# A recurrent-attention and expert kernel: the gate's count of every fourth chunk behind the block product instead of ahead of the scores

## Chip, cores, metric

One core of one Trainium2 chip. The metric is the device time of one execution in microseconds (us); lower is better. The inputs are fixed; the output is a float32 array of 3072 x 320.

## What is computed

Three stages follow one another. The first is a recurrence over 768 steps for 32 (batch, head) pairs with a 40 x 40 state; its output is 3072 tokens of 320 features. The second sends each token to the best of 8 experts (with a capacity), two matrix products per expert. The third is a dense layer pair with a squared ReLU. Cut to what matters:

```python
for t in range(S):                       # S = 768, state is B x H x 40 x 40
    y[:, :, t] = einsum('bhd,bhde->bhe', rt, state)
    Sa = einsum('bhde,bhe->bhd', state, at)
    state = state * wt[:, :, None, :] - einsum('bhd,bhe->bhde', Sa, bt) \
            + einsum('bhd,bhe->bhde', vt, kt)
...
expert_idx = argmax(x @ w_gate, axis=1)  # and gate_w, its softmax weight
# token i goes to place counts[e] of its expert e, in order of i
...
h = maximum(disp @ w1[e], 0); y = h @ w2[e]; out[i] = gate_w[i] * y[e, pos[i]]
...
h = maximum(x @ w_in, 0); return (h * h) @ w_out
```

## The kernel before, in words

The recurrence is done in 24 chunks of 32 steps (`Attention.run`). A chunk's coefficients form 32 x 32 triangular blocks, one for each of the 32 pairs, that have to be inverted. Their inverse is built by VectorE for four chunks at once, in pieces that are laid into the chunks between other work (`inv`, L265 and L269), and ends with a transpose into `TT` (L304). The index m = c % 4 tells a chunk's place in such a group; in the fourth chunk (m = 3) the inverse is ready and the next group's first block is taken from it.

All engines issue in the order in which the program is written (a manual schedule). `chunk(c)` (L585) is the body for chunks 1 to 19. The names that matter here, in the order of one chunk:

- `u(c)`: 32 small products into `pu` (L399), four copies to `vu` by ScalarE (L404).
- `y(c - 1)`: the last chunk's output into the PSUM tile `py` (L489).
- `nat_k(c + 1)` (L341, `pk`) and `gram(c + 7)`: the Gram products `G` (L192) of a chunk seven ahead, which VectorE masks into `GM` and `N` (L205, L206).
- `state(c)` (L418, `ps`) and `vu_t(c)`: transposes `pv` (L455) and two copies to `vut` by ScalarE (L458).
- `block_T(c + 1)`: four copies `TB` from `TT` by ScalarE (L313). In the fourth chunk they stand behind `vu_t`, since `TT` is made only then.
- `gate.count` of a batch of chunks: an exponential (L895), four matmuls into the PSUM tile `pc` (L899; the profile shows eight pieces), a copy to `pr` (L901).
- `scan` and `scale` (coefficients of chunk c + 8: two scans on VectorE, three products on POOL, L178), `state_decay(c)` (L429), `gate_in(c - 1)`: VectorE reads `py` and writes the token rows `xt` (L498).
- `scores(c)`: 16 matmuls into `pq` (L467; 32 pieces), masked by VectorE (`scores_mask`, L475).
- `solve(c + 1)`: the block product `px` of `TB` and `X` (L385), and two copies to `lu` by ScalarE (L388), which the next chunk's `u` needs.
- `gate.xT(c - 1)`: transposes `gpt` of `xt` (L845) and copies `gxT` (L847); `nat_a` (`pa`, L341), `state_t` (`pn`, L441), `gate.logits` (`pl`, L861).
- on VectorE at the end: pieces of the inverse (m below 3), or the rank of a batch of tokens (L908 to L938), which needs `pr`.

Batches for the gate are chunks 0-1, 2-5, 6-9, 10-13, 14-16 and later ones; a batch's count comes two chunks behind its last chunk, so for the first four it is in chunks 3, 7, 11 and 15, all with m = 3. In those it is called ahead of the scan (`early`); the later ones stand behind `gate.xT` already.

PSUM tiles come from two pools. Large ones (`pu`, `pk`, `G`, `ps`, `pv`, `px`, `pa`, `pn`) take three buffers in turn. Small ones (`py`, `pc`, `pq`, `gpt`, `pl`) take two buffers in turn, in the order in which they are asked for:

```python
def small(self, nm):
    self.ns += 1
    return self.ps1.tile([128, 512], F32, tag=f"s{self.ns % 2}", name=nm)
```

A tile can be written only when the last reader of the tile before it in that buffer has ended. The functions that the change touches, and what calls them:

Of the kernel before, what the change touches and what calls it, by code (L numbers as in the profile page):

```python
# [35 lines left out]
class Attention:  # L36
# [476 lines left out]
    def run(self, extra, weights):  # L513
# [3 lines left out]
        gate = self.gate  # L517

        def fill(c, i):
            if 1 <= c <= 2:  # L520
                extra(5 * c + i, 5 * c + i + 1)
            elif 5 <= c < 14 and i == 2:
                extra(10 + c, 11 + c if c < 13 else None)

        def wload(i):
            r = (self.L, self.Tt)[i % 2].rearrange("p a b -> p (a b)")
            weights.load(i, r[:, 0:704], 1)
# [57 lines left out]
        def chunk(c):  # L585

            m, bt = c % 4, gate.batch(c)
            plan = FIRST if c < 4 else PLAN
            early, nxt = bt if c < 17 else None, gate.batch(c + 1) if c < 16 else None
            self.u(c)  # L590
            if bt and 17 <= c:
                gate.choose(*bt)
            self.y(c - 1)
            self.nat_k(c + 1)
            if m != 3:
                self.block_T(c + 1)
            self.load_r(c + 1)
            self.load(c + LA + 2, 0)
            fill(c, 0)
            self.gram(c + LA)  # L600
            self.gram_mask(c + LA)
            self.state(c)
            self.vu_t(c)
            if m == 3:
                self.block_T(c + 1)
            self.load(c + LA + 2, 1)
            fill(c, 1)
            if early:
                gate.count(*early)
            self.scan(c + LA + 1)  # L610
            self.scale(c + LA + 1)
            self.state_decay(c)
            self.gate_in(c - 1)
            self.scores(c)
            self.scores_mask(c)
            if m == 0:
                self.inv_start(c // 4 + 1, lambda k, h: G)
            self.solve(c + 1)
            self.load_v(c + 2)
            self.store_x(c - 1)  # L620
            self.load_w(c + LA + 4)
            self.load(c + LA + 2, 2)
            fill(c, 2)
            gate.xT(c - 1)
            if bt and 17 <= c:
                gate.count(*bt)
            self.nat_n(c + 2)
            self.nat_a(c + 2)
            self.nat_pc(c + 2)
            self.state_t(c + 1)  # L630
            self.load(c + LA + 2, 3)
            fill(c, 3)
            gate.logits(c - 1)
            if m != 3:
                self.inv("v" * plan[m])
            if nxt:
                gate.choose(*nxt)
            if m == 2:
                self.inv("v" * plan[3])
            if bt:  # L640
                gate.rank(*bt)
                gate.rank_batch(*bt)
            fill(c, 4)
            gate.scatter(1)
            if c == 19:
                wload(0)
                wload(1)
# [5 lines left out]
        for c in range(NC - 1):  # L653
            if 1 <= c < SHIFT:
                chunk(c)
                continue
# [1014 lines left out]
```

## Time and profile before

| | |
|---|---|
| median of 3 runs | 1120.45 us (1119.92 to 1125.08) |
| the profiled execution | 1126.1 us, its span 1124.2 us |
| instructions in it | 30643 |
| mean granted TensorE clock | 0.904 of full speed |
| busy share: PE, DVE, ACT, POOL | 83%, 69%, 50%, 24% |
| chain that ended last: PE, DVE, DMA, issue, ACT | 54%, 18%, 6%, 6%, 5% |

PE is TensorE's matmul stream, DVE VectorE, ACT ScalarE. Busy shares are means over all of it. The chain follows the end back through what released each step; "issue" is time in which the engine waited for nothing that the profile shows. A row of the timeline gives the start and length in us, the engine, the line and what it writes and reads; several equal instructions in a row are merged (x32), and the bracket tells how long the engine was idle before and what released it. A wait for several things is put down to the one that came last by the profile, which can be the wrong one.

### The profile page before, as it was taken

How to read it: one execution, taken by the hardware profiler on the slowest of the kernel's cores; microseconds unless marked ns; L12 is line 12 of the kernel's file. 1: busy time of each engine (PE TensorE's matmuls, PEld its weight loads, DVE VectorE, ACT ScalarE, POOL GpSimd, SP SyncE). 2: the span in 40 equal slices, each digit the busy share in tenths (PEclk: the TensorE clock that was granted, in tenths of full speed). 3: DMA queues.
4: the chain of work that ended last, by engine and by line, in shares of the span. 5: the costliest groups of instructions: out<-in, count | busy, mean ns of one | idle time of the engine just before them, and what ended most of it. 6: DMA issues, size and time to landing. Idle time of an engine off the chain costs nothing.

```text
span 1124.2 us, 30643 instructions
## 1 busy us (share of the span) xinstructions
PE 934.6 (83%) x12526; PEld 842.7 (75%) x12526; DVE 774.2 (69%) x1611; ACT 560.4 (50%) x1286; POOL 273.8 (24%) x320
## 2 busy tenths in 40 slices
PE   5247677778666788889889999799999999999995
PEld 3237566667665677768879999798899999999895
DVE  7999979889798795465887888876644344444432
ACT  7135464555463767634545566546634343434432
POOL 5422131222313101013554555423401010000000
PEclk6578888797797988899989999999999999999998
DMA  7736544444442223236765666534100001000000
GB/s 184 194 97 184 172 125 124 124 140 149 115 149 84 87 61 104 79 93 181 222 209 187 208 212 216 178 98 143 50 24 24 24 12 37 1 24 2 19 5 27
DMA packets 80647, 122.71 MB, mean 109 GB/s; under 512 B 9679, under 2 KB 57409, under 8 KB 79561
## 3 DMA queue, kind: packets, MB, share of 16 engines
q1 hardware_dynamic: 71173, 100.09, 30.2%
q10 hardware_dynamic: 7020, 12.78, 3.8%
q0 software_dynamic: 2304, 7.78, 2.2%
q8 instruction: 101, 1.65, 0.6%
q14 instruction: 49, 0.40, 0.1%
HBM read 91.36 MB, written 29.35 MB: 107 GB/s over the span
## 4 chain that ended last, share of the span: by engine, by line
PE 54%; DVE 18%; DMA 6%; issue 6%; ACT 5%; POOL 1%; SPq 1%; ACTq 0%; DVEq 0%; POOLq 0%
PE phg L1334 15%; PE phe L1334 5%; PE pog L1359 5%; PE pog L1360 5%; PE pog L1358 5%; DVE pr L265 4%; PE px L385 3%; DMA xs<-zs_s 2%; PE pq L467 2%; PE poe L1360 2%; PE poe L1358 2%; PE poe L1359 2%; DVE Tt L269 1%; DVE ru L429 1%; DVE Xm L269 1%
## 5 line engine op out<-in xcount | busy, mean ns | idle before, releaser
L1344 DVE SCALAR_TENSOR_TENSOR sqg<-phg,rg 128x512 f32<-128x512 f32 x96 | 66.2, 690 | 119.0 <-ACT rg L1343 119.0
L1343 ACT ACTIVATE rg<-phg 128x512 f32<-128x512 f32 x96 | 57.2, 596 | 110.5 <-PE phg L1334 110.3
L1346 DVE TENSOR_TENSOR hlg<-sqg,hhg 128x512 fp32r<-128x512 f32 x96 | 66.5, 693 | 65.9 <-ACT hhg L1345 63.2
L1345 ACT CAST hhg<-sqg 128x512 fp32r<-128x512 f32 x96 | 59.6, 621 | 78.5 <-DVE sqg L1344 78.5
L1334 PE MATMUL phg<-xhg,e 128*128 128x512 f32 x264 | 93.1, 393 | 0.0
L385 PE MATMUL px<-TB,X 128*104 128x128 f32 x384 | 67.2, 347 | 26.2 <-ACT TB L313 25.0
L388 ACT COPY lu<-px 104x512 f32<-104x512 f32 x48 | 25.7, 588 | 120.5 <-PE px L385 120.5
L385 PEld LDWEIGHTS px<-TB,X 128*104 128x104 f32 x384 | 61.7, 230 | 28.8 <-ACT TB L313 25.4
L467 PE MATMUL pq<-rq,vut 128*64 128x64 f32 x768 | 42.1, 264 | 49.0 <-issue 31.7
L178 POOL TENSOR_TENSOR e<-e 104x512 f32<-104x512 f32 x21 | 27.9, 1331 | 207.4 <-DVE e L163 90.2
L467 PEld LDWEIGHTS pq<-rq,vut 128*64 128x64 f32 x768 | 35.7, 173 | 55.0 <-issue 32.2
L1359 PE MATMUL pog<-e,hhg 128*128 128x320 f32 x240 | 74.1, 309 | 0.0
L1360 PE MATMUL pog<-e,hlg 128*128 128x320 f32 x240 | 74.1, 309 | 0.0
L1358 PE MATMUL pog<-e,hhg 128*128 128x320 f32 x240 | 73.9, 308 | 0.0
L192 PE MATMUL G<-e 64*32 64x64 f32 (+1 forms) x1536 | 27.6, 254 | 49.3 <-issue 29.2
L192 PEld LDWEIGHTS G<-e 64*32 64x32 f32 (+1 forms) x1536 | 20.1, 120 | 59.3 <-issue 33.6
L1152 POOL TENSOR_TENSOR e<-rw,e 128x256 fp32r<-128x256 f32 x51 | 43.0, 846 | 72.3 <-ACT e L1151 71.5
L1334 PE MATMUL phe<-xhe,e 128*128 128x480 f32 (+4 forms) x176 | 59.3, 378 | 0.0
L178 POOL TENSOR_TENSOR e<-e,wB 104x512 f32<-104x512 f32 x42 | 53.4, 1287 | 24.3 <-DVE wB L157 17.1
L1334 PEld LDWEIGHTS phg<-xhg,e 128*128 128x128 f32 x264 | 49.5, 188 | 8.8
L313 ACT COPY TB<-TT 32x256 f32<-32x256 f32 x94 | 37.8, 402 | 35.6 <-DVE TT L304 34.3
L1338 ACT ACTIVATE hhe<-phe 128x480 fp32r<-128x480 f32 (+4 forms) x64 | 33.9, 529 | 38.7 <-PE phe L1334 38.2
(315 smaller groups left out, 2919.5 us busy)
## 6 DMA issues: line engine op xcount, KB each, us to landing
e<-in_E_dram ACTq DMA_DIRECT2D x60, 208.0 KB
rw<-in_w_dram SPq DMA_DIRECT2D x30, 320.0 KB
zs_s<-zt SPq DMA_DIRECT2D x24, 320.0 KB
rw<-in_w_dram SPq DMA_DIRECT2D x30, 256.0 KB
e<-in_E_dram SPq DMA_DIRECT2D x9, 832.0 KB
ru<-in_VR_dram SPq DMA_DIRECT2D x48, 128.0 KB
cr<-in_wi_dram SPq DMA_DIRECT2D x20, 256.0 KB
cr<-in_wo_dram SPq DMA_DIRECT2D x20, 256.0 KB
```

Source lines behind the costliest of these rows:

```text
L178: eng.tensor_tensor(z, z, f, ALU.mult)
L192: T.matmul(gps[32 * g : 32 * g + 32, par, 64 * o : 64 * o + 64], e[r, 32 * i : 32 * i + 32], e[r, 512 + 64 * i : 576 + 64 * i], start=True ...
L385: self.nc.tensor.matmul(px[0:104, par, 128 * o : 128 * o + 128], X[:, par, o, :], TB[:, 4 * par + o, :], start=True, stop=True)
L467: T.matmul(pq[s, 64 * q : 64 * q + 64], vut[:, q, s], rt[:, :, q, pp], start=True, stop=True)
L1334: T.matmul(o, lt, rt, start=(i == 0), stop=(i == len(seq) - 1))
L1343: A.activation(r[:, :n], o, AF.Relu)
L1344: V.scalar_tensor_tensor(sq[:, :n], o, 0.0, r[:, :n], ALU.max, ALU.mult)
L1345: A.copy(hh[:, :n], sq[:, :n])
L1346: V.tensor_tensor(hl[:, :n], sq[:, :n], b32(hh)[:, :n], ALU.subtract)
L1358: T.matmul(o, hh[:, t], W["h2"], start=(f == 0), stop=False)
L1359: T.matmul(o, hh[:, t], W["l2"], start=False, stop=False)
L1360: T.matmul(o, hl[:, t], W["h2"], start=False, stop=(f == NF - 1))
```

## The change

The call of `gate.count` for the batches of chunks 3, 7, 11 and 15 moves from ahead of `scan` to behind `solve`. Nothing else is edited.

```diff
--- before.py
+++ after.py
@@ -605,8 +605,6 @@
                 self.block_T(c + 1)
             self.load(c + LA + 2, 1)
             fill(c, 1)
-            if early:
-                gate.count(*early)
             self.scan(c + LA + 1)
             self.scale(c + LA + 1)
             self.state_decay(c)
@@ -616,6 +614,8 @@
             if m == 0:
                 self.inv_start(c // 4 + 1, lambda k, h: G)
             self.solve(c + 1)
+            if early:
+                gate.count(*early)
             self.load_v(c + 2)
             self.store_x(c - 1)
             self.load_w(c + LA + 4)
```

TensorE in chunk 11, from the end of `vu_t` to the transposes of the gate. `pc6` is the count, `pq11` the scores, `px12` the block product, `gpt10` the transposes; the brackets name what an instruction waits for. Before:

```order
L455 MATMUL pv11_4353<-ident0_59,vu1_115 80x64 [waits PE_49,Activation_49]
L455 MATMUL pv11_4353<-ident0_59,vu1_115 80x64 x15
L899 MATMUL pc6_4378<-oh_412,mats_384 128x32 [waits DVE_49]
L899 MATMUL pc6_4378<-oh_412,mats_384 128x32 x3
L467 MATMUL pq11_4397<-rq1_119,vut_117 64x64 [waits DMAHW0_49,DMAHW6_49,DVE_49,Activation_49]
L467 MATMUL pq11_4397<-rq1_119,vut_117 64x64 [waits Activation_49]
L467 MATMUL pq11_4397<-rq1_119,vut_117 64x64 x14
L385 MATMUL px12_4416<-TB0_110,X0_106 104x128 [waits PE_49,Activation_49]
L385 MATMUL px12_4416<-TB0_110,X0_106 104x128 x7
L845 MATMUL gpt10_4436<-ident0_59,xt10_4395 128x128 [waits Activation_49]
```

Now:

```order
L455 MATMUL pv11_4353<-ident0_59,vu1_115 80x64 [waits PE_49,Activation_49]
L455 MATMUL pv11_4353<-ident0_59,vu1_115 80x64 x15
L467 MATMUL pq11_4389<-rq1_119,vut_117 64x64 [waits DMAHW6_49,DMAHW0_49,Activation_49]
L467 MATMUL pq11_4389<-rq1_119,vut_117 64x64 [waits Activation_49]
L467 MATMUL pq11_4389<-rq1_119,vut_117 64x64 x14
L385 MATMUL px12_4408<-TB0_110,X0_106 104x128 [waits DVE_49,PE_49,Activation_49]
L385 MATMUL px12_4408<-TB0_110,X0_106 104x128 x7
L899 MATMUL pc6_4420<-oh_412,mats_384 128x32 [waits DVE_49]
L899 MATMUL pc6_4420<-oh_412,mats_384 128x32 x3
L845 MATMUL gpt10_4436<-ident0_59,xt10_4387 128x128 [waits DVE_49,PE_49]
```

The count's four matmuls stand behind the block product. The first scores matmul no longer waits for VectorE (`DVE`); the block product, the count and the first transpose of the gate do, each for a buffer or an operand.

ScalarE in the same chunk, from the last copies of `TB` on. Before:

```order
L313 COPY TB0_110<-TT_109 32x8x32 [waits DVE_49]
L313 COPY TB0_110<-TT_109 32x8x32 x3
L138 DMA e4_4282<-in_E_dram 104x512 [waits DMAHW2_49]
L895 ACTIVATE ex_6_4177<-d_6_4176 128x32
L901 COPY pr_6_4383<-pc6_4378 128x128 [waits PE_49]
L388 COPY lu_116<-px12_4416 104x512 [waits PE_49,Activation_49]
L388 COPY lu_116<-px12_4416 104x512 [waits Activation_49]
L138 DMA e4_4282<-in_E_dram 104x512 [waits DMAHW0_49]
L847 COPY gxT10_4440<-gpt10_4436 128x256 [waits PE_49]
```

Now:

```order
L313 COPY TB0_110<-TT_109 32x8x32 [waits DVE_49]
L313 COPY TB0_110<-TT_109 32x8x32 x3
L138 DMA e4_4282<-in_E_dram 104x512 [waits DMAHW2_49]
L388 COPY lu_116<-px12_4408 104x512 [waits PE_49,Activation_49]
L388 COPY lu_116<-px12_4408 104x512 [waits Activation_49]
L895 ACTIVATE ex_6_4177<-d_6_4176 128x32
L901 COPY pr_6_4425<-pc6_4420 128x128 [waits PE_49]
L138 DMA e4_4282<-in_E_dram 104x512 [waits DMAHW6_49]
L847 COPY gxT10_4440<-gpt10_4436 128x256 [waits PE_49]
```

The exponential (`ex`) and the counts' copy (`pr`) stand behind the two copies of the block product (`lu`), and ahead of a load's issue (L138) and of the copies of the gate's transposes (`gxT`). The orders of VectorE, POOL and SP have the same rows as before, in the same places.

## Rows read from the trace of the kernel before

**Rows 1.** One line of the kernel, L901 (the copy of the counts): who waited for it.

```profile
  PE pq L467: 28.7, 4
```

**Rows 2.** Timeline, chunk 11: start us, us, engine, line, operation, xcount [idle before <-releaser].

```profile
280.17 1.07 ACT L458 COPY vut<-pv 80x512 f32<-80x512 f32 x2 [2.01 <-PE pv L455]
...
282.95 1.23 ACT L313 COPY TB<-TT 32x256 f32<-32x256 f32 x3
...
287.77 0.49 DVE L498 TENSOR_TENSOR xt<-py,Pn 128x320 f32<-128x320 f32 x1
...
288.36 1.97 PE L467 MATMUL pq<-rq,vut 128*64 128x64 f32 x32 [6.81 <-issue]
...
290.26 3.63 PE L385 MATMUL px<-TB,X 128*104 128x128 f32 x16
...
290.37 1.39 DVE L475 TENSOR_TENSOR rq<-pq,mQ 64x512 f32<-64x512 f32 x2 [2.11 <-PE pq L467]
...
293.73 0.49 PE L845 MATMUL gpt<-ident,xt 128*128 128x128 f32 x3
...
295.90 0.80 PE L399 MATMUL pu<-ru,lu 128*32 128x40 f32 x64
```

**Rows 3.** Timeline, chunk 12, which has no count: scores and gate_in.

```profile
305.48 1.15 PE L467 MATMUL pq<-rq,vut 128*64 128x64 f32 x30 [0.15 <-ACT vut L458]
...
306.42 0.49 DVE L498 TENSOR_TENSOR xt<-py,Pn 128x320 f32<-128x320 f32 x1
```

**Rows 4.** Timeline, chunks 3, 7 and 15: count, gate_in, transpose, first product of the next.

```profile
132.52 1.38 PE L899 MATMUL pc<-oh,mats 128*128 128x16 f32 x8
...
142.31 0.49 DVE L498 TENSOR_TENSOR xt<-py,Pn 128x320 f32<-128x320 f32 x1
...
147.63 0.49 PE L845 MATMUL gpt<-ident,xt 128*128 128x128 f32 x3
...
149.80 0.80 PE L399 MATMUL pu<-ru,lu 128*32 128x40 f32 x64
...
214.78 0.49 DVE L498 TENSOR_TENSOR xt<-py,Pn 128x320 f32<-128x320 f32 x1
...
219.75 0.49 PE L845 MATMUL gpt<-ident,xt 128*128 128x128 f32 x3
...
221.92 0.80 PE L399 MATMUL pu<-ru,lu 128*32 128x40 f32 x64
...
361.39 0.49 DVE L498 TENSOR_TENSOR xt<-py,Pn 128x320 f32<-128x320 f32 x1
...
366.40 0.49 PE L845 MATMUL gpt<-ident,xt 128*128 128x128 f32 x3
...
368.58 0.80 PE L399 MATMUL pu<-ru,lu 128*32 128x40 f32 x64
```

**Rows 5.** VectorE's waits, 290 to 300 and 296 to 356: us, times, longest.

```profile
DVE rq L475 <- PE pq L467: 2.1, 1, 2.1
...
DVE GM L205 <- PE G L192: 5.1, 1, 5.1
```

**Rows 6.** Timeline, chunks 12 and 13: the Gram matmuls behind the first product.

```profile
300.21 0.93 PE L192 MATMUL G<-e 64*32 64x64 f32 x52 [1.77 <-issue]
...
310.56 0.80 PE L399 MATMUL pu<-ru,lu 128*32 128x40 f32 x64
...
315.57 0.75 PE L192 MATMUL G<-e 64*32 64x64 f32 x52 [2.36 <-issue]
```

**Rows 7.** Timeline, from chunk 6 into chunk 7: transpose, first product, Gram matmuls.

```profile
196.74 0.55 PE L845 MATMUL gpt<-ident,xt 128*128 128x128 f32 x3 [2.89 <-DVE xt L498]
...
199.42 1.29 PE L399 MATMUL pu<-ru,lu 128*32 128x40 f32 x64
...
204.98 0.85 PE L192 MATMUL G<-e 64*32 64x64 f32 x35 [2.05 <-issue]
```

**Rows 8.** Stretches, TensorE, chunk 11: us, PE busy (x), granted clock, DMA share, GB/s.

```profile
283.50:293.60 10.10, 5.24 (x48) 0.50 0.32 89
```


## Prediction

> **What bounds the kernel now.** I read the chain of waits first (which engine the end hangs on, stage by stage), then the timeline of the four chunks that the change touches, then VectorE's list of waits, then the granted clock.
>
> In the chunk stage the chain runs through VectorE for most of a group of four chunks (the inverse of a 32x32 block, in pieces) and crosses to TensorE once per group: in the fourth chunk, 3, 7, 11 and 15. There the list of who waited for whom says that the matmuls of `scores` stood still for 28.7 us in 4 waits, and names ScalarE's copy of the gate's counts [rows 1]. The timeline of chunk 11 says otherwise [rows 2]. ScalarE had written the last of `vut`, the operand of `scores`, by 281.24 (280.17 + 1.07) and the last of `TB` by 284.18 (282.95 + 1.23). The first matmul of `scores` starts at 288.36, 0.10 us after VectorE ends `gate_in` (287.77 + 0.49 = 288.26). In chunk 12, which has no count, `scores` runs from 305.48, ahead of `gate_in` at 306.42 [rows 3]. So what ends the wait is `gate_in`.
>
> The code says why. The small PSUM tiles alternate between two buffers. In a chunk without a count they come as `py`, `pq`, `gpt`, `pl`: `pq` gets the other buffer than `py`. The count puts `pc` between `py` and `pq`, so `pq` gets `py`'s buffer, and `py` is read by `gate_in`, which stands behind two scans and the state's decay on VectorE. The order of TensorE shows it too: the first `scores` matmul waits for VectorE in this chunk.
>
> VectorE pays twice. It waits 2.1 us for `scores` to mask them, and later 5.1 us for the next chunk's Gram matmuls; from there to the next group's fourth chunk it waits for nothing else of size [rows 5]. So what moves those Gram matmuls earlier moves the whole group, until VectorE's own 2.1 + 5.1 = 7.2 us are used up.
>
> **The change, step by step.** Each of the four chunks issues the same instructions: 4 matmuls (8 pieces), an exponential, a copy. None is added, no DMA is added, SP's and POOL's orders are the same. What differs:
>
> 1. *`scores` is freed.* `pq` now takes the buffer of the last chunk's `pl`, long free. It needs `vut` only: about 281.3 instead of 288.36 in chunk 11. At the price it has now, 1.97, it ends near 283.3.
> 2. *The block product `px`* then waits for `TB` (284.18), and through its own buffer for the Gram mask, which VectorE has done just after `TB` starts. It takes 3.63 at the clock it has now, so it ends by 287.8 at the latest, still ahead of `gate_in`. ScalarE's copies of `lu` follow it there. All of this leaves the path.
> 3. *The count is the new follower of `gate_in`:* `pc` now gets `py`'s buffer. It starts where `scores` used to, 288.36. In chunk 3 all of it took 1.38 [rows 4], the dearest price there is, so it ends by 289.74.
> 4. *The transpose `gpt`* is behind the count, and it now gets `pq`'s buffer, so it waits for the mask of the scores. VectorE does that mask right behind `gate_in`, without its 2.1 us of waiting: 1.39 [rows 2]. So `gpt` starts about 0.10 + 1.39 = 1.49 after `gate_in` ends, at 289.75, level with the count's end. Now it starts at 293.73: 3.98 earlier.
> 5. *What stands behind the wait of the count:* on TensorE `gpt`, the transposes, logits and then `pu` of the next chunk, all of which needed `gate_in` or the mask anyway. On ScalarE one DMA issue for `E` and the copy of `gpt`, both earlier than now. On VectorE the rank, which needs the counts' copy: shortly behind 289.74, where now it begins behind the mask at 291.76 (290.37 + 1.39). No cost.
>
> The same for the other three [rows 4], with `gate_in` ending 0.49 after `xt` starts:
> - chunk 3: 142.31 + 0.49 + 1.49 = 144.29 against 147.63: 3.34
> - chunk 7: 214.78 + 0.49 + 1.49 = 216.76 against 219.75: 2.99
> - chunk 15: 361.39 + 0.49 + 1.49 = 363.37 against 366.40: 3.03
>
> With chunk 11 that is 13.3 us. `pu` follows `gpt` by 2.17 in chunk 11 (293.73 to 295.90) and is moved by as much. None of the four is over the 7.2 us that VectorE has to give.
>
> Whether it reaches VectorE hangs on a gap: the Gram matmuls of chunk 12 stop for 1.77 and go on at 300.21, released by nothing that the profile shows [rows 6]. They go on 4.31 after `pu` starts (295.90); in chunk 13 they go on 5.01 after it (310.56 to 315.57). The gap follows `pu`, not a load, so I take it to move along.
>
> **The unknown cost is the clock.** [...] Afterwards there are three shorter stops in place of one long one (about 1 ahead of `px`, up to 2 ahead of the count, and a fraction ahead of `gpt`), and I can't read off whether the burst from `gpt` to the Gram matmuls then falls into a slow stretch. Below, the price is nothing: it runs as now. Above, the step into chunk 7 shows it: after a wait of 2.89, `gpt` to `pu` took 2.68 (196.74 to 199.42), not 2.17, and from `pu` to the point where the Gram matmuls go on 5.56 (to 204.98), not the 4.31 of chunk 12 [rows 7]. That is 0.51 + 1.25 = 1.76 a chunk, 7.0 in all. I take one chunk of the four as slow: its wait of 2.89 is longer than any stop that I expect. That is 1.8.
>
> [...]
>
> **Sum.** 13.3 - 1.8 = 11.5. The profiled execution took 1126.1 with a span of 1124.2 and would take 1114.6; it lies 5.65 above the median of the three runs. From the median: 1120.45 - 11.5 = **1109.0**. After chunk 15 nothing is fixed in time that I can find: each later stage's loads are issued behind its own work, so the end moves with it.
>
> **The rivals.**
> - *The clock takes half of it.* All four bursts fall into a slow stretch: 13.3 - 7.0 = 6.3, so 1114.2. For it: [rows 7]. Against: now a stop of nearly 7 us costs the burst behind it nothing, because `scores` and `px` take the slow stretch; shorter stops should do less.
> - *The gap ahead of the Gram matmuls doesn't move.* If it ends with something fixed in time, VectorE starts the next group when it does now and only chunk 15, with no full group behind it, may give its 3.0: between 1117.4 and 1120.5. For it: the profile names no releaser. Against: it trails `pu` by 4.3 and 5.0 in chunks where `pu` comes at different points.
> - *Slower: `scores` isn't freed.* If another piece of VectorE's work (the state's decay, say) rather than the shared buffer held `scores`, it would still start 0.1 after `gate_in`, and the count would stand behind `px` on the path, where now it lies in the wait. Its price is 1.38 each time: 4 x 1.38 = 5.5 slower, 1126.0. It decides from the point where `scores` starts behind `gate_in` again. For it: the profile's list names another releaser altogether [rows 1]. Against: the 0.10 us of [rows 2], and the new order, in which the first `scores` matmul of these chunks waits for no VectorE instruction.
> - *The change does nothing that it says* can be excluded for the order (it is shown above), not for the effect; that is the second rival.
>
> **How the numbers follow.** Forecast 0.67, with its own range from none slow (1107.1) to three slow bursts (1112.4). The clock rival 0.16, the gap that stays 0.10, slower 0.05, the rest 0.02. Half a per cent is 5.6 us, about what a measurement of this kernel can tell from no change. Faster by more than that (under 1114.8) are the forecast and nearly all of the clock rival: 0.82. Within it are the gap that stays, the rest, and part of the slower rival, which lies at the bound itself: 0.15. Slower: 0.03. The range goes from 1105.0 (none slow, and some 2 us from bursts that now are slow elsewhere, as the one into chunk 7) to 1114.5 (all four slow).
>
> **What would show it.** Right: in chunks 3, 7, 11 and 15 `scores` starts just behind `vut`, before `gate_in`; VectorE's wait for it (4 times 2.1) is gone; the count starts 0.1 behind `gate_in`, `gpt` about 1.5 behind it; `pu` of the next chunk follows `gate_in` by some 3.7 instead of 7 and more; the first expert starts about 11 us earlier and lasts as long as now. Wrong: `scores` still behind `gate_in`; or the Gram matmuls of chunks 4, 8, 12 and 16 no nearer to `gate_in`; or the granted clock at 0.50 while `gpt` to `pu` run in all four; or an earlier end of the chunks and a longer stage behind them.

## The result and the profile after

| | before | with the change |
|---|---|---|
| median (20 runs each) | 1123.55 us (1113.79 to 1129.8) | 1111.99 us (1106.14 to 1120.98) |
| profiled execution, its span | 1126.1, 1124.2 us | 1111.7, 1109.8 us |
| ratio | | 0.9909, 95% interval 0.9887 to 0.993 |

The change makes the kernel faster by 0.9%. The three runs known beforehand lay at the low side of the 20: against their median the ratio gives 0.9909 x 1120.45 = 1110.3 us, 10.2 less. The two medians in the table are 11.6 apart, a ratio of 0.9897; the 0.9909 is nearer to the ratio of the means, and the 10.2 is the figure used below. The page of the profile after, its span, busy shares and chain:

```profile
span 1109.8 us, 30634 instructions
...
PE 937.4 (84%) x12526; PEld 842.1 (76%) x12526; DVE 774.2 (70%) x1611; ACT 562.8 (51%) x1286; POOL 274.5 (25%) x320
...
PE 47%; DVE 30%; DMA 8%; issue 7%; ACT 4%; POOL 3%; SPq 1%; ACTq 0%; DVEq 0%; POOLq 0%
```

VectorE's part of the chain was 18% and is 30%, and TensorE's was 54% and is 47%. Where that happens is seen in the timeline after, chunk 11, which answers to [rows 2] and to the first line of [rows 6]:

```profile
277.42 1.07 ACT L458 COPY vut<-pv 80x512 f32<-80x512 f32 x2 [4.22 <-PE pv L455]
278.06 2.46 PE L467 MATMUL pq<-rq,vut 128*64 128x64 f32 x32 [0.76 <-ACT vut L458]
...
280.67 2.84 PE L385 MATMUL px<-TB,X 128*104 128x128 f32 x16 [0.15 <-ACT TB L313]
...
284.20 0.49 DVE L498 TENSOR_TENSOR xt<-py,Pn 128x320 f32<-128x320 f32 x1
284.61 1.38 DVE L475 TENSOR_TENSOR rq<-pq,mQ 64x512 f32<-64x512 f32 x2
...
284.74 1.08 PE L899 MATMUL pc<-oh,mats 128*128 128x32 f32 x8 [1.24 <-DVE xt L498]
...
286.13 0.87 PE L845 MATMUL gpt<-ident,xt 128*128 128x128 f32 x3 [0.31 <-DVE rq L475]
...
289.88 1.29 PE L399 MATMUL pu<-ru,lu 128*32 128x40 f32 x64
...
294.78 0.73 PE L192 MATMUL G<-e 40*32 40x64 f32 x49 [1.19 <-issue]
...
295.55 0.42 DVE L205 TENSOR_TENSOR GM<-G,mM 128x256 f32<-128x256 f32 x1 [4.87 <-PE G L192]
```

`scores` (L467) starts behind the copies of `vut`, 6.6 us ahead of the end of `gate_in` (284.69), and no longer 0.10 behind it. The count starts 0.05 behind `gate_in`, the transpose `gpt` 1.44 behind it, where it was 5.47. But from `gpt` to `pu` it takes 3.75 us now, where [rows 2] has 2.17.

VectorE's list of waits over the stage (100 to 385 us: total, times, longest) answers to [rows 5]. Before:

```profile
DVE GM L205 <- PE G L192: 17.8, 4, 5.1
DVE rq L475 <- PE pq L467: 11.0, 6, 2.2
```

After:

```profile
DVE GM L205 <- PE G L192: 15.0, 4, 4.9
DVE rq L475 <- PE pq L467: 2.7, 2, 1.7
```

VectorE's waits became 11.1 us shorter, 8.3 for the scores and 2.8 for the Gram matmuls. The first expert's transposes start 11.6 us earlier (493.9 to 482.3). The experts last 254.7 and 252.0 us; in these and the later runs they take 249.3 to 254.7, whatever was edited. The dense stage takes 375.6 and 375.5. So the change's own gain lies ahead of the experts, and the 14.4 us between the two profiled executions are partly chance.

The 11.6 is not all the change's either. From the transpose into `TT` in chunk 3 to the Gram mask of chunk 16, the stretch that holds all four chunks, it is 238.3 us before and 229.2 with the change, 9.0 less. The transpose itself came 1.4 later. From that mask to the first expert it took 120.6 us and then 116.6, 4.0 less, and this stretch differs by as much between two executions of one kernel (114.6 in e2_held, 119.7 in e7_held_again, which is e2_held again).

### The profile page after: what moved, and what is told of

It reads as the page before. It is cut to its first block, busy times and chain, and to the rows that moved or that the text cites. A ratio compares the mean times of both kernels' runs of the same rounds, so it can differ in the third digit from the quotient of the medians.

```text
span 1109.8 us, 30634 instructions
## 1 busy us (share of the span) xinstructions
PE 937.4 (84%) x12526; PEld 842.1 (76%) x12526; DVE 774.2 (70%) x1611; ACT 562.8 (51%) x1286; POOL 274.5 (25%) x320
## 3 DMA queue, kind: packets, MB, share of 16 engines
q8 instruction: 101, 1.65, 0.6%
## 4 chain that ended last, share of the span: by engine, by line
PE 47%; DVE 30%; DMA 8%; issue 7%; ACT 4%; POOL 3%; SPq 1%; ACTq 0%; DVEq 0%; POOLq 0%
PE phg L1334 16%; DVE pr L265 5%; PE pog L1360 5%; PE pog L1359 5%; PE pog L1358 5%; PE phe L1334 3%; DVE ru L429 2%; DMA e<-in_E_dram 2%; DVE Tt L269 2%; DVE Xm L269 2%; DVE rq L475 2%; DVE e L163 2%; POOL ct L1072 2%; DMA xs<-zs_s 2%; DVE wB L157 1%
## 5 line engine op out<-in xcount | busy, mean ns | idle before, releaser
L467 PE MATMUL pq<-rq,vut 128*64 128x64 f32 x768 | 37.5, 237 | 22.3 <-ACT vut L458 21.2
L1360 PE MATMUL poe<-e,hle 128*120 128x320 f32 (+4 forms) x150 | 47.3, 315 | 6.8 <-DVE hle L1339 6.7
L467 PEld LDWEIGHTS pq<-rq,vut 128*64 128x64 f32 x768 | 30.8, 147 | 29.3 <-ACT vut L458 27.3
```

The costliest lines, as they stand in the source:

```text
L467: T.matmul(pq[s, 64 * q : 64 * q + 64], vut[:, q, s], rt[:, :, q, pp], start=True, stop=True)
L1360: T.matmul(o, hl[:, t], W["h2"], start=False, stop=(f == NF - 1))
```

## The experiments

These readings decide nearly everything. They are taken in chunks 3, 7, 11 and 15 of each profiled execution and added up: from the end of `gate_in` to the start of `gpt`; from there to the start of `pu`; from there to the start of the next chunk's Gram mask `GM`, where VectorE is let on. The last is split into the stops of TensorE without a releaser and the rest. In us, over the four chunks:

| kernel | `gate_in` to `gpt` | `gpt` to `pu` | `pu` to `GM`, without stops | such stops | sum |
|---|---|---|---|---|---|
| before | 19.30 | 8.69 | 13.75 | 6.48 | 48.22 |
| the change | 6.10 | 12.32 | 17.15 | 2.75 | 38.32 |
| e1_flip | 5.15 | 8.98 | 15.72 | 6.31 | 36.16 |
| e2_held | 22.68 | 8.84 | 15.97 | 3.94 | 51.43 |
| e3_flip_ahead | 1.76 | 9.02 | 15.20 | 7.32 | 33.30 |
| e4_warm | 6.82 | 10.38 | 16.10 | 5.10 | 38.40 |
| e5_shift | 6.11 | 14.10 | 19.78 | 0.41 | 40.40 |
| e7_held_again | 25.00 | 8.83 | 15.74 | 4.51 | 54.08 |

The expectations name theories by letters. A: the shared small buffer held `scores`. B: the count's place ahead of them did, whatever the buffers. C: the granted clock behind `gate_in` sets how much of the gain arrives. F: the stops without a releaser are TensorE's supply of instructions.

### e1_flip: the buffer alone, the count where it was

```diff
             if early:
                 gate.count(*early)
+                self.ns += 1
             self.scan(c + LA + 1)
```

One turn of the small buffers is skipped, so `pq` gets the count's buffer and not `py`'s.

> The count stays ahead of the scores, as in the kernel before; one turn of the two small buffers is skipped behind it, so that the scores tile takes the count's buffer and not that of the last output. Theory A (the shared buffer held the scores): scores start just behind the copy of the counts, some 3.5 us ahead of gate_in in chunks 3, 7, 11 and 15; VectorE's wait of 2.1 for them is gone; from the end of gate_in to the Gram mask of the next chunk the four take 36 to 42 us together (before 48.2, after 38.3); ratio to before 0.987 to 0.994. Theory B (the count's place ahead of the scores costs, whatever the buffer): scores still 0.1 behind gate_in, 48 us together, ratio 0.998 to 1.002.

Measured: 1113.16 us (6 runs) against 1126.04 (17), ratio 0.9888 (0.9868 to 0.9908). Its timeline, chunk 11:

```profile
279.19 1.97 PE L467 MATMUL pq<-rq,vut 128*64 128x64 f32 x32 [2.29 <-ACT pr L902]
281.09 2.66 PE L385 MATMUL px<-TB,X 128*104 128x128 f32 x16
281.50 0.49 DVE L498 TENSOR_TENSOR xt<-py,Pn 128x320 f32<-128x320 f32 x1
...
283.59 0.49 PE L846 MATMUL gpt<-ident,xt 128*128 128x128 f32 x3
```

`scores` waits for the copy `pr` (now truly, it reads the shared buffer) and starts 2.8 us ahead of the end of `gate_in` (281.99). The count was not moved, and the whole gain is there. B is out: the place cost time through the buffer.

### e2_held: the count moved, the buffer shared again

Against the change:

```diff
             self.gate_in(c - 1)
+            if early:
+                self.ns += 1
             self.scores(c)
```

> The change, but with one turn of the small buffers skipped ahead of the scores in chunks 3, 7, 11 and 15, so that the scores take the buffer of the last output again. Theory A (buffer): scores 0.1 behind gate_in again, VectorE waits 2.1 for them again, and the count now lies on the path behind the block product: 48.2 + 4 x 1.1 = about 52.6 us from gate_in to the next Gram mask in the four together; ratio 1.002 to 1.006, slower than before. Theory B (place): as the change, 38 us, ratio 0.989 to 0.993.

Measured: 1124.55 us (12 runs), ratio 0.9978 (0.995 to 1.0007). Its timeline, chunk 11:

```profile
287.64 0.49 DVE L498 TENSOR_TENSOR xt<-py,Pn 128x320 f32<-128x320 f32 x1
288.24 2.08 PE L467 MATMUL pq<-rq,vut 128*64 128x64 f32 x32 [8.75 <-issue]
...
293.64 0.98 PE L901 MATMUL pc<-oh,mats 128*128 128x32 f32 x8
...
294.46 0.53 PE L847 MATMUL gpt<-ident,xt 128*128 128x128 f32 x3
```

`scores` is back at 0.1 behind `gate_in` (288.13), in all four chunks, and the count lies on the path: `gpt` comes 6.33 behind. The sum to `GM` is 51.43 us, 3.2 over before. The gain is gone, as A says, but the whole time came out below the 1.002 to 1.006 that A expected; e7 repeats it.

### e3_flip_ahead: the buffer, and the count earlier still

Against before, the count goes ahead of the copies `TB`, with the skipped turn:

```diff
             self.vu_t(c)
+            if early:
+                gate.count(*early)
+                self.ns += 1
             if m == 3:
                 self.block_T(c + 1)
...
-            if early:
-                gate.count(*early)
             self.scan(c + LA + 1)
```

> The count behind vu_t and ahead of the block copies of TB, and one turn of the small buffers skipped behind it: the scores wait only for the copy of the counts, which ScalarE makes right behind vut, and the transposes of the gate get the last output's buffer, so they need gate_in and not the mask. Theory A: scores about 0.5 behind the end of vut, the block product ends ahead of gate_in, gpt about 0.1 behind gate_in, 1.4 sooner than in the change; the four stretches from gate_in to the next Gram mask 32 to 36 us together (38.3 in the change); ratio 0.983 to 0.989, below the change. Theory B: no better than before, 48 us, ratio 0.998 to 1.002.

Measured: 1109.49 us (6 runs), ratio 0.9853 (0.9819 to 0.9887). Its timeline, chunks 11 and 12:

```profile
278.09 1.47 PE L900 MATMUL pc<-oh,mats 128*128 128x32 f32 x6
...
279.91 1.98 PE L467 MATMUL pq<-rq,vut 128*64 128x64 f32 x32 [0.36 <-ACT pr L902]
281.82 3.74 PE L385 MATMUL px<-TB,X 128*104 128x128 f32 x16
283.73 0.49 DVE L498 TENSOR_TENSOR xt<-py,Pn 128x320 f32<-128x320 f32 x1
...
285.36 0.56 PE L846 MATMUL gpt<-ident,xt 128*128 128x128 f32 x3
...
292.67 1.06 PE L192 MATMUL G<-e 40*32 40x64 f32 x50 [1.19 <-issue]
```

The count fills the time before `scores`, so nothing stands between `gate_in` and `gpt` but the block product: in chunks 3 and 15 `gpt` starts 0.05 behind `gate_in`, in chunk 7 0.52 and in this one 1.14, behind `px`. TensorE's pause ahead of that burst is 0.33 in chunk 3, 0.55 in chunk 15 and none in the other two, and `gpt` to `pu` takes 9.02 in all, not 12.32. This version has the lowest ratio, 0.9853 against the change's 0.9909. Its interval touches the change's at 0.9887 and overlaps those of e1 and e4, so that it is the fastest is shown in the stage (33.30 us, the least sum) and not in the whole time.

### e4_warm: the clock of the burst

Against the change, three useless matmuls are put ahead of the block product, into its own buffer, in the four chunks:

```diff
...
         px = self.big(f"px{c}")
+        for i in range(fill):
+            self.nc.tensor.matmul(px[:, i % 2, 0:256], self.idle[:, 0:128], self.idle[:, 0:256], start=True, stop=True)
...
-            self.solve(c + 1)
+            self.solve(c + 1, 3 if early else 0)
```

> The change, with three matmuls of 128x256 without use put ahead of the block product in chunks 3, 7, 11 and 15, while it waits for TB (they write the product's own tile, which it then overwrites). Theory C (part of the gain is lost to the lower clock, which the stops of TensorE ahead of the block product and the count bring on): gpt to pu takes about 2.2 to 2.7 in all four, 9 to 10 together (12.3 in the change, 8.7 before), the stretches from gate_in to the next Gram mask 35 to 37 us together (38.3); ratio 0.986 to 0.991. Rival D (the length of that burst has another cause than those stops): gpt to pu 11.5 or more together, 38 to 40 us, ratio 0.990 to 0.994.

Measured: 1112.26 us (6 runs), ratio 0.9882 (0.9859 to 0.9904). The granted clock is read in stretches from the start of `gpt` to that of `pu` in the four chunks; those of before are 3.0 us long and go on 0.8 past it (us, TensorE busy, its weight loads, VectorE, ScalarE, POOL, clock, DMA share, GB/s). Before:

```profile
147.60:150.60 3.00, 3.00 (x134) 2.78 (x136) 1.81 (x13) 2.69 (x10) 1.18 (x1) 1.00 0.43 124
219.70:222.70 3.00, 3.00 (x129) 2.79 (x132) 2.56 (x17) 2.67 (x10) 1.01 (x1) 1.00 0.49 143
293.70:296.70 3.00, 3.00 (x134) 2.78 (x136) 2.00 (x14) 2.69 (x10) 1.01 (x1) 1.00 0.43 132
366.40:369.40 3.00, 3.00 (x137) 2.78 (x139) 2.56 (x17) 2.72 (x10) 1.01 (x1) 1.00 0.03 5
```

With the change:

```profile
146.10:149.80 3.70, 3.70 (x52) 3.29 (x52) 2.67 (x17) 2.39 (x9) 1.19 (x1) 0.50 0.44 154
216.20:218.80 2.60, 2.60 (x53) 2.35 (x54) 2.19 (x13) 2.03 (x8) 0.43 (x1) 0.76 0.69 195
286.20:289.80 3.60, 3.60 (x51) 3.21 (x51) 3.02 (x18) 2.10 (x8) 1.28 (x2) 0.50 0.71 219
358.80:360.90 2.10, 2.10 (x51) 1.90 (x51) 1.76 (x10) 1.59 (x8) 0.41 (x1) 1.00 0.22 71
```

With e4_warm:

```profile
142.00:144.10 2.10, 2.10 (x51) 1.91 (x51) 1.76 (x11) 1.75 (x9) 0.31 (x1) 1.00 0.58 162
212.00:215.70 3.70, 3.70 (x51) 3.31 (x51) 3.12 (x18) 2.21 (x9) 1.38 (x2) 0.50 0.70 223
285.00:287.10 2.10, 2.10 (x52) 1.90 (x51) 1.05 (x6) 2.08 (x10) 0.00 (x0) 1.00 0.76 243
355.20:357.30 2.10, 2.10 (x51) 1.90 (x51) 1.76 (x9) 1.55 (x7) 0.43 (x1) 1.00 0.23 72
```

Before, the granted clock was 1.00 in all four bursts. With the change two run wholly at 0.50 and a third partly (1.00 from 216.2 to 217.4 us, 0.50 from 218.0 to 218.8, 0.76 in the mean); with the useless matmuls three of four run at 1.00, and chunk 7 at 0.50. Yet the sum to `GM` is 38.40 us, no better than 38.32. By the table `gpt` is 0.7 later, the matmuls from `gpt` to `GM` take 1.9 + 1.1 = 3.0 less, and the stops without a releaser take 2.4 more. So the burst was long because of the lower clock, as C says, and D is out: at 1.00 it takes 2.20 to 2.21 us, in chunk 7 at 0.50 3.76, 10.38 together. But C's forecast of 35 to 37 us for the sum failed. What the faster clock gave back, a later start of `gpt` and longer stops took. The whole time tells nothing: its interval overlaps the change's.

### e5_shift: what the stops are

Against the change, 24 small useless matmuls are put at the start of the program, far ahead of all that is compared:

```diff
+        self.warm(24, self.zt, 8, True)
```

> The change, with 24 more matmuls of 8 columns without use at the start, while TensorE waits for the first load: 48 matmul pieces with 48 weight loads, so that every later instruction of TensorE stands 48 pieces further on in its stream. Theory F (TensorE stops ahead of the Gram matmuls' rest because its next block of instructions isn't there: a block is 128 matmul pieces with their weight loads, and 16 KB of instructions land about 1.5 us before each such stop ends): the stops without a releaser move 48 pieces back; in chunk 12 from piece 15 of the Gram matmuls into py, at about its piece 39, and from piece 14 of pv into ps, at about its piece 30; none is left within the Gram matmuls of chunks 9 to 16. Rival G (the stop belongs to the Gram matmuls: an operand or a buffer of theirs): it stays within the Gram matmuls. Whole time by either: ratio 0.986 to 0.995, as the change, give or take what the stops then cost elsewhere.

Measured: 1113.94 us (10 runs) against 1124.23 (23), ratio 0.9903 (0.9875 to 0.9931): the time stays that of the change. With the change, the same chunk's stop stands behind the 15th piece of the Gram product:

```profile
310.45 0.34 PE L192 MATMUL G<-e 64*32 64x64 f32 x15
312.45 0.73 PE L192 MATMUL G<-e 40*32 40x64 f32 x49 [1.67 <-issue]
```

With e5_shift it stands behind the 41st piece of `py`, and the page counts 48 more matmul pieces than the 12526 above:

```profile
PE 951.1 (85%) x12574; PEld 856.0 (77%) x12574; DVE 774.4 (69%) x1611; ACT 563.0 (50%) x1286; POOL 274.3 (25%) x320
...
305.36 0.57 PE L489 MATMUL py<-rhsY,rq 128*32 128x40 f32 x41
308.39 0.63 PE L489 MATMUL py<-rhsY,rq 128*32 128x40 f32 x23 [2.46 <-issue]
308.95 1.65 PE L341 MATMUL pk<-ident,e 104*128 104x104 f32 x8
310.53 1.18 PE L192 MATMUL G<-e 64*32 64x64 f32 x64
```

From the 41st piece of `py` to the 15th of `G` there are 23 + 8 + 15 = 46 pieces: the stop came earlier in the program by about as many as were added at its start, and the Gram product runs through. Nowhere between 80 and 460 us of that execution does a stop of over 0.55 us without a releaser stand in a Gram product, where the change has 14; they stand in `py` and `ps`. So the stop belongs to a count of issued instructions, not to an operand of `G`. The count shows in another way too: with the change, four Gram stops (those that end at 294.78, 327.57, 345.2 and 364.61 us) have their next stop in `pv`, and each time 127 recorded pieces lie between the two. That these stops are waits for instructions is inferred from the transfers. The page after counts 101 of them on a queue of kind "instruction". Each of the 14 Gram stops of the change and each of the 16 of before (over 0.55 us, 80 to 460 us) ends 2.0 to 3.0 us after one such transfer has begun; before, the stop that ends at 300.21 [rows 6] has its transfer between 297.7 and 298.9 us:

```profile
q8 instruction: 101, 1.65, 0.6%
```

```profile
q8 instruction: 1, 0.02, 5.1%
```

The first line is from the page after, the second from the DMA view of before in that stretch. 12526 pieces with as many weight loads are 25052 instructions, 248 to a transfer, if that queue serves TensorE alone. Not every transfer stops it: with the change 64 begin between 80 and 460 us, and 19 stops of over 0.55 us without a releaser stand there, 14 of them in Gram products. F stands. The sum is no shorter for it: 40.40 us, with almost no stops in these stretches but with slow bursts (14.10 from `gpt` to `pu`, three of them 3.75 to 3.76 long, as the one of chunk 11 at 0.50 with the change).

### e6_all_held: the same sharing in the other chunks

Against before:

```diff
             self.gate_in(c - 1)
+            if not early:
+                self.ns += 1
             self.scores(c)
```

> The kernel before, with the order unchanged; one turn of the small buffers is skipped ahead of the scores in all chunks of the same body that have no count ahead of them (15 chunks), so that there too the scores take the buffer of the last output. Theory A (the buffer): in those chunks scores start 0.1 behind gate_in, and VectorE, which bounds those chunks, waits some 2.1 for them each time: 15 x 2.1 = 31 us, with the block product pushed behind as well; ratio 1.02 to 1.04. Theory B (the count's place): nothing changes, ratio 0.998 to 1.002.

Measured: 1155.49 us (4 runs), ratio 1.027 (1.0216 to 1.0323), 30.4 us slower. VectorE's list of waits for the scores, 0 to 520 us. Before:

```profile
DVE rq L475 <- PE pq L467: 19.4, 9, 3.1
```

With e6_all_held (the second line is chunk 12, whose releaser the profile doesn't show):

```profile
DVE rq L475 <- PE pq L467: 45.2, 21, 3.1
DVE rq L475 <- issue: 2.1, 1, 2.1
```

The waits for the scores grow by 45.2 + 2.1 - 19.4 = 27.9 us, nearly all of the difference. Every one of the 15 chunks waits now, 13 of them 1.7 to 2.2 us longer than before; chunk 8 waited 0.28 before, and chunk 16, with 2.17 before and 1.29 now, gains. The price of one sharing is the wait for the scores, and it can be put in and taken out at will.

### e7_held_again: e2 once more

The kernel of e2_held.

> The kernel of e2_held once more (the change, with scores held by the last output's buffer), since its four chunks were longer than before by about 3 us and its whole time was not. From the transpose into TT in chunk 3 to the Gram mask of chunk 16, theory A expects 241 us again (238.3 before, 229.2 with the change). If the whole is 2 to 4 us over before's, the first time was chance; if it is again 2 us or more below, something behind chunk 16 gains in this kernel, by theory A unexplained.

Measured: 1125.74 us (12 runs), ratio 1.0015 (0.9985 to 1.0045). The sum to `GM` is 54.08 us, 5.9 over before. From the transpose in chunk 3 to the Gram mask of chunk 16 it takes 244.4 us, not 241 (e2_held 241.0), and the whole is 1.5 over before's median, less than the 2 to 4 expected. What e2_held made good it made good behind chunk 16: 114.6 us from there to the first expert, where before took 120.6, and this time 119.7. The two together show a kernel that is not faster than before; that it is slower can be seen in the stage, not in the whole time.

## Why the prediction was right, and where it was off

- *What held `scores`.* Right. The profile names ScalarE's copy [rows 1]; the order of the buffers named `gate_in`, and e1, e2 and e6 show it by undoing the sharing, restoring it and adding it elsewhere.
- *Steps 1 and 2.* Right: `scores` 6.6 to 7.7 us ahead of the end of `gate_in`, `px` done ahead of it in all four chunks.
- *Step 3.* Right in place, 0.05 to 0.06 behind `gate_in`. In chunk 3 the count took 1.89 us, over the 1.38 taken as its dearest price [rows 4], and there `gpt` came 1.78 behind `gate_in`.
- *Step 4.* Right: 1.44 in the three others, 1.49 predicted. Together `gpt` gained 19.30 - 6.10 = 13.2 us; the sum had 13.3.
- *Step 5.* Right: VectorE's only new wait is 0.4 us, for the counts' copy.
- *The clock.* This is the term that was mis-sized, "one chunk of the four as slow", 1.8. Two bursts run wholly at a granted clock of 0.50 and one partly (0.76 in the mean). `gpt` to `pu` takes 12.32 instead of 8.69, 3.6 more, and the rest up to `GM`, stops aside, 17.15 instead of 13.75, 3.4 more. That is 7.0, and that it equals the figure taken as the upper bound is chance. The bound was 1.76 for each of four chunks, 0.51 of it between `gpt` and `pu`; a burst wholly at 0.50 took 1.6 more there, and chunks 3, 7, 11 and 15 lost 2.7, 1.3, 2.5 and 0.5. Nor is all of it shown to be the clock. The 3.6 is, by the granted clock and e4. Of the 3.4, 0.5 fell in chunk 15, where the granted clock was 1.00 throughout (358.8 to 365.7 us), and in e1 the same reading is 15.72, 2.0 over before, though `pk` takes 0.93 to 0.94 there in all four chunks and 0.93 before, at 1.00; what that rest is stays open. The sentence "its wait of 2.89 is longer than any stop that I expect" was no reason. The longest pauses between `scores` and `gpt` were 2.08, 1.12, 1.24 and 1.05 us, and the bursts behind them ran at 0.50, 0.76, 0.50 and 1.00.
- *The gap ahead of the Gram matmuls.* It was taken to follow `pu`, and mostly does, but it isn't constant: the stops went from 6.48 to 2.75 us, 3.7 less. With the change a transfer of instructions ran between 151.0 and 152.3 us, at a granted clock of 0.50, under `py` and `pk` behind chunk 3 (1.29 and 1.22 long, where before they take 0.79 and 0.93), and no stop followed it. That a slower burst hides more of a transfer is an inference from the table: e4, where three bursts run at 1.00, has 5.10 of stops, e1, with 8.98 from `gpt` to `pu`, 6.31, and e5, with 14.10 there, 0.41. But e2 and e7, with 8.84 and 8.83 there, have only 3.94 and 4.51, so where the stops fall matters as well, and how much the clock alone moves them stays open.

So the two errors are of opposite sign: 13.2 - 7.0 + 3.7 = 9.9 us at the Gram masks, where 13.3 - 1.8 = 11.5 was forecast. The runs gave 10.2 and VectorE's waits 11.1. That the forecast came this near is in part luck: the matmuls lost about four times what was set down for them, and the shorter stops, which the sum did not have, made up for more than half of it. The absolute time, 1109.0 forecast and 1111.99 measured, differs mostly because the median of before rose from 1120.45 to 1123.55 with more runs. The first expert starts 11.6 earlier, where some 11 was said, but only 9.0 of that arose in the chunks of the change; the stages behind it last as before, within their own spread. The clock rival named a loss of the right size, and would have had 6.3 us arrive; it lacked the shorter stops.

Not tried: taking the instruction stops away altogether, which would show what the clock alone is worth in the whole time.

## What to carry to other kernels

Where tiles take buffers in turn, one tile more between two others changes who shares with whom: look at which reader the late starter's buffer is waiting for, by the order of the buffers, before believing the releaser that a profile names. Skipping one turn (e1) gave what moving the call gave, and skipping it with the call placed in idle time (e3) gave more in the stage. Add up a gain at the place where the engine that bounds the stage is let on, not where the wait was removed.

## What the runs showed of the hardware

In the chunk stage, where it runs many small matmuls (64 pieces in 0.80 us for `pu`), TensorE stops at some of the transfers of its instructions, as inferred in e5: with the change, 14 times for 0.60 to 4.54 us ahead of pieces of the Gram product, at points that are set by the count of instructions (48 pieces more at the start put chunk 12's stop 46 pieces earlier in the program) and not by what stands there. The 101 transfers move 1.65 MB, 16 KB each, and 248 matmul pieces and weight loads come to one by the estimate in e5. Of 64 that begin between 80 and 460 us some 19 show as stops of over 0.55 us, so most of them cost less than that; but where the cost shows it isn't small, by the stops above. A second surprise was how little of a faster clock arrives: with three bursts wholly at 1.00 instead of one (e4), the matmuls gained 3.0 us and longer stops took 2.4.
